# Attention and MLP in one kernel: more of v loaded, k copied and biased in another order, and a new plan of order and loads

## The chip, the cores and the metric

The kernel runs on one core of a Trainium2 chip. The metric is device time in microseconds (us) of one execution of the whole program; lower is better. The engines are TensorE (PE in the profile: matmuls), VectorE (DVE), ScalarE (ACT), GpSimd (POOL) and SyncE (SP). POOL and SP compute little here; they issue the DMAs, POOL the loads and SP the stores and the DMA transposes.

## The reference

Sliding-window attention feeds a two-layer MLP. Inputs and output are f32.

```python
# q, k, v: (8 batches, 8 heads, 576 positions, 64)
scores = (1 / 8) * q @ k.T                      # per batch and head
mask = (rel >= 0) & (rel < 64)                  # rel = query position - key position
attn = softmax(where(mask, scores, -1e9))
x = (attn @ v).transpose(0, 2, 1, 3).reshape(4608, 512)
h = x @ w_in                                    # 512 x 2048
return (h * sigmoid(h)) @ w_out                 # 2048 x 512
```

## The kernel before

**Attention** runs in blocks of 64 queries; a block needs its own 64 keys and the 64 before. A batch has 9 blocks, so there are 72 blocks and 18 units of 4 blocks. A unit goes through: scores on PE (L372 for units 0 to 4, L349 for the others), exponent on ACT (L378), mask on VectorE (L381; units 0 and 1 instead get a large negative bias, which PE adds before the scores with `window` or `window0` and `ident`, L363), values on PE ("pv", L412 or L400), reciprocal and norm on VectorE (L417, L420). Then the result is turned into `bridge`, the MLP's input with features on the partitions: for units in the set `BACK` by four PE transposes for each half (L436) and a copy (L439), for all others by a DMA transpose that SP issues (L430).

**The MLP** runs in 9 tiles of 512 tokens, two units to a tile. The first layer (L444) reads `bridge` and the whole of w_in, 8 loads of 256 columns each; ACT applies silu (L450). Tile 0 has a plain second layer (L513); tiles 1 to 5 have the second layer by seven products of sums (L517, sums of silu's output `gs` on VectorE, L505), and tiles 6 to 8 also the first layer (L481, with sums of `bridge`, L472). L878 adds up the output of tiles 1 and later.

**Loads.** All go through POOL's queue. q and k come for single units up to unit 4 (L297) and for half batches afterwards (L261, L274), with the positions on the partitions; VectorE turns them (L303, L316). For units 0 to 4 the keys of the block before are copied beside each block's own, 32 partitions at a time, by ACT or VectorE (`shift_k`, L292 and L294; r is the block of the unit). v needs 128 keys on the partitions for each block. Blocks 1, 3, 5, 7 and 8 of a batch are loaded so (`load_v`, L320, 128 KB each), and VectorE fills the even blocks from these (`shift_v`, L340 and L342). At most 8 loads are under way: POOL issues the next one when the one eight before it has landed. v has three buffers (NVB), so v of a batch waits until the batch three before is done with.

**The order** on every engine is fixed when the kernel is built. `Plan` simulates the engines with an estimated duration for each step, and at each moment gives a free engine the ready step of the lowest rank; each engine then executes the list that results, in order. `rank` gives each kind of step a number, `GO` says after how many MLP matmuls each unit's scores may come, and `SEQ` is the order of the first loads: a to e are k and q of units 0 to 4, v and y v of batches 0 and 1, w and o the eighths of w_in and w_out.

Of the kernel before, what the change touches and what calls it, by code (L numbers as in the profile page):

```python
# [124 lines left out]
def kernel(ctx, tc, q, k, v, w_in, w_out, out):  # L125
    nc = tc.nc
# [4 lines left out]
    NB = S // 64  # L131
# [10 lines left out]
    BACK = {0, 1, 2, 3, 5}  # L142
    GO = [52, 40, 40, 212, 232, 280, 393, 376, 440, 320, 585, 624, 56, 762, 352, 460]
# [7 lines left out]
    UP = 4  # L151
    LATE = [0, 0, 1, 3, 4, 4, 4, 4]
# [59 lines left out]
    def pair(op):  # L212
# [5 lines left out]
        rank=dict(one=-9, first=-9, late=5, dma=-1, st=-2, kshift=-0.5, xo=-20.9, turn=16.7, shift=34.1,  # L218
                  s=15.9, exp=-16.5, mask=9.4, pv=17.0, inverse=-18.6, norm=-28.3, ot=-1.2, bridge=-21.7,
                  silu=8.6, moe=99, warm=200, sum=4.1, xsum=-37.3, asum=15.9, plus=-31.0, stage=-0.9, wsum=7.8, piece=-29.3, out=-2.0, prime=-8,  # L220
                  turn2=-9.4, turn1=-26.9, shift0=-4.0, shift0b=27.1, shift1=36.9, inverse0=-5.3, norm0=-1.5, bridge0=16.8,),
# [34 lines left out]
    c_vv = [p.add("one", {"DVE": 0.4}, lambda _, i=i: clear_vv(i)) for i in range(NVB)]  # L256
    c_zero = p.add("one", {"DVE": 0.1}, lambda _: nc.vector.memset(zero, 0.0))
# [8 lines left out]
    def add_consts():  # L266
        c_ident = p.add("dma", {"POOL": 0.6}, const_ident)
        c_window = p.add("dma", {"POOL": 0.8}, const_window)
        c_window0 = p.add("one", {"DVE": 0.3}, const_window0, [c_window])
        return c_ident, c_window0, p.add("late", {"DVE": 0.8}, const_mask, [c_window])  # L270
# [48 lines left out]
    def load_v(b, t):  # L319
        nc.gpsimd.dma_start(  # L320
            out=vv[b % NVB][:, t, :, 0:D],
            in_=v[b, :, 64 * t - 64:64 * t + 64].rearrange("h s d -> s h d"),
        )
# [247 lines left out]
    def add_v(b, ts, shifts):  # L571
        users = pv_last.get(b - NVB, []) + [c_vv[b % NVB]]
        for t in ts:
            v_done[b, t] = [p.add("dma", {"POOL": 1.0}, lambda _, t=t: load_v(b, t), users,
                                  dma=0.9 if b < 2 else 1.35, late=1.5 * (t > 3) if b < 2 else LATE[b] + VLATE * (b > 2))]
        for low, a, z in shifts:
            n = len(range(a, z, 2))
            sh = p.add("shift", {"DVE": 0.1 + 0.22 * n}, lambda e, low=low, a=a, z=z: shift_v(e, b, low, a, z),
# [439 lines left out]
```

## Time and profile before

| | |
|---|---|
| median of 3 runs | 284.39 us (283.83, 284.39, 284.41) |
| the profiled execution | 283.85 us |
| its span in the profile | 282.1 us |
| mean granted clock of PE | 0.987 |
| busy: PE, VectorE, ACT, POOL | 272.2, 206.3, 172.7, 109.4 us |
| the chain that ended last | PE 85%, DMA 9%, POOL 2%, others 1% or less each |
| DMA | 32.52 MB in 106885 packets, 115 GB/s over the span |

A row of the timeline reads: start and length in us, engine, line, operation, output and inputs, how many instructions are taken together, and in brackets the idle time before them with what ended it. A row of the table by windows has the stretch, its length, the busy time of each engine with its count of instructions, PE's granted clock, the DMA engines' share and GB/s. Matmul ends are modelled, so a busy PE can hide short gaps. A page on DMAs gives for each kind of load the count, the size and the median from issue to landing.

### The profile page before, as it was taken

How to read it: one execution, taken by the hardware profiler on the slowest of the kernel's cores; microseconds unless marked ns; L12 is line 12 of the kernel's file. 1: busy time of each engine (PE TensorE's matmuls, PEld its weight loads, DVE VectorE, ACT ScalarE, POOL GpSimd, SP SyncE). 2: the span in 40 equal slices, each digit the busy share in tenths (PEclk: the TensorE clock that was granted, in tenths of full speed). 3: DMA queues.
4: the chain of work that ended last, by engine and by line, in shares of the span. 5: the costliest groups of instructions: out<-in, count | busy, mean ns of one | idle time of the engine just before them, and what ended most of it. 6: DMA issues, size and time to landing. Idle time of an engine off the chain costs nothing.

```text
span 282.1 us, 8326 instructions
## 1 busy us (share of the span) xinstructions
PE 272.2 (96%) x3509; PEld 192.9 (68%) x3509; DVE 206.3 (73%) x384; ACT 172.7 (61%) x266; POOL 109.4 (39%) x163
## 2 busy tenths in 40 slices
PE   8499999999999999999999999999999999999995
PEld 4376445545884478645875488547888888888884
DVE  5863468899967689797697657858587867868641
ACT  2486855786558686575847675666556664555631
POOL 8966847728998688873670000000000000000000
PEclk9869999999999999999999999999999999999999
DMA  8999999999999999999999202440013001201303
GB/s 82 155 195 189 185 185 184 199 245 137 131 197 181 147 130 163 171 190 129 144 158 197 40 0 78 121 69 0 2 37 99 16 22 66 67 0 40 114 30 119
DMA packets 106885, 32.52 MB, mean 115 GB/s; under 512 B 91488, under 2 KB 105824, under 8 KB 106848
## 3 DMA queue, kind: packets, MB, share of 16 engines
q0 software_dynamic: 83360, 19.15, 78.3%
q1 hardware_dynamic: 23488, 12.85, 20.8%
q8 instruction: 27, 0.44, 0.7%
q14 instruction: 10, 0.08, 0.1%
HBM read 38.27 MB, written 9.44 MB: 169 GB/s over the span
## 4 chain that ended last, share of the span: by engine, by line
PE 85%; DMA 9%; POOL 2%; issue 1%; ACT 1%; DVE 1%; POOLq 0%; DVEq 0%
PE mp L517 29%; PE mp L444 24%; PE la L481 8%; PE la L517 6%; PE mp L513 5%; PE mp L481 5%; DMA w_out_sb<-in_moe_w_out_dram 3%; PE at L349 3%; DMA nat<-in_k_dram 3%; PE at L400 3%; DMA nat<-in_q_dram 2%; PE at L412 1%; POOL nat L297 1%; PE at L372 1%; POOL vv L320 1%
## 5 line engine op out<-in xcount | busy, mean ns | idle before, releaser
L444 PE MATMUL mp<-bridge,w_in_sb 128*128 128x512 bf16 (+1 forms) x408 | 87.3, 367 | 0.8 <-issue 0.4
L450 ACT ACTIVATE gt<-mp 128x512 bf16<-128x512 f32 (+1 forms) x102 | 56.9, 573 | 24.2 <-PE mp L444 23.6
L444 PEld LDWEIGHTS <-w_in_sb 128*128 128x128 bf16 x408 | 38.7, 98 | 41.4 <-issue 1.4
L517 PEld LDWEIGHTS <-gs 128*128 128x128 bf16 x512 | 49.5, 98 | 5.9
L378 ACT ACTIVATE eo<-at 128x1024 bf16<-128x1024 f32 x34 | 33.6, 1026 | 14.1 <-PE at L349 8.7
L517 PE MATMUL mp<-ws,gs 128*128 128x256 bf16 x320 | 39.9, 273 | 0.0
L320 POOL DMA_DIRECT2D vv<-in_v_dram x40 | 35.6, 901 | 6.2 <-DMA nat<-in_k_dram 2.1
L517 PEld LDWEIGHTS <-gt 128*128 128x128 bf16 x288 | 27.5, 98 | 4.4
L274 POOL DMA_DIRECT2D nat<-in_q_dram x40 | 24.2, 623 | 15.6 <-DMA vv<-in_v_dram 9.1
L381 DVE TENSOR_TENSOR eo<-eo,mask 128x1024 bf16<-128x1024 bf16 x32 | 21.3, 677 | 8.0 <-ACT eo L378 7.9
L875 ACT COPY ot<-mp 128x512 f32<-128x512 f32 (+1 forms) x28 | 15.8, 563 | 18.6 <-PE mp L517 17.2
L274 POOL DMA_DIRECT2D nat<-in_k_dram x40 | 24.3, 628 | 3.8 <-DMA nat<-in_k_dram 1.3
L505 DVE TENSOR_TENSOR gs<-gt 128x1024 bf16<-128x1024 bf16 x24 | 16.5, 686 | 10.2 <-ACT gt L450 10.2
L492 ACT ACTIVATE eo<-vv 128x512 bf16<-128x512 f32 (+1 forms) x18 | 13.9, 773 | 16.2 <-DVE vv L766 16.2
L420 DVE TENSOR_TENSOR eo<-at,rc 128x512 bf16<-128x512 f32 x36 | 23.1, 670 | 0.2
L517 PE MATMUL mp<-w_out_sb,gt 128*128 128x256 bf16 x176 | 22.6, 273 | 0.0
L878 DVE TENSOR_TENSOR ot<-mp,ot 128x512 f32<-128x512 f32 (+1 forms) x21 | 13.8, 657 | 6.9 <-PE mp L517 5.7
L513 PE MATMUL mp<-w_out_sb,gt 128*128 128x512 bf16 x64 | 15.7, 380 | 0.0
L766 DVE TENSOR_TENSOR vv<-mp,vv 128x512 f32<-128x512 f32 x15 | 10.3, 688 | 7.1 <-PE mp L481 7.1
L766 DVE TENSOR_TENSOR vv<-la,vv 128x512 f32<-128x512 f32 x21 | 13.7, 682 | 2.0 <-PE la L481 1.7
L481 PEld LDWEIGHTS <-w_in_sb 128*128 128x128 bf16 x144 | 14.1, 98 | 1.6
L517 PE MATMUL mp<-w_out_sb,gs 128*128 128x256 bf16 x112 | 14.4, 273 | 0.0
(117 smaller groups left out, 397.1 us busy)
## 6 DMA issues: line engine op xcount, KB each, us to landing
out_dram<-ot SPq DMA_DIRECT2D x32, 256.0 KB, 3.6
vv<-in_v_dram POOLq DMA_DIRECT2D x40, 128.0 KB, 6.4
nat<-in_k_dram POOLq DMA_DIRECT2D x40, 72.0 KB, 5.4
nat<-in_q_dram POOLq DMA_DIRECT2D x40, 72.0 KB, 4.6
w_in_sb<-in_moe_w_in_dram POOLq DMA_DIRECT2D x8, 256.0 KB, 8.7
w_out_sb<-in_moe_w_out_dram POOLq DMA_DIRECT2D x8, 256.0 KB, 8.6
out_dram<-ot SPq DMA_DIRECT2D x8, 128.0 KB, 1.7
nat<-in_k_dram POOLq DMA_DIRECT2D x3, 256.0 KB, 6.3
```

Source lines behind the costliest of these rows:

```text
L274: nc.gpsimd.dma_start(out=nats[i].bitcast(BF16)[32 * r:32 * r + 32].rearrange("s (g y) -> s g y", y=128), in_=(q, k)[kk][b, h].rearrange(" ...
L320: nc.gpsimd.dma_start(out=vv[b % NVB][:, t, :, 0:D], in_=v[b, :, 64 * t - 64:64 * t + 64].rearrange("h s d -> s h d"),)
L378: nc.scalar.activation(out=dst, in_=src, func=ACTF.Exp, scale=scale)
L381: nc.vector.tensor_mul(es[w], es[w], mask)
L420: nc.vector.tensor_mul(oxs[o].rearrange("p x c (r d) -> p x (c r) d", r=2), at_pv(op, hf)[:, :, :, 0:D], rcs[r].unsqueeze(3).to_broadcast( ...
L444: nc.tensor.matmul(bank(bk)[:, lo:hi], lhsT=w_in_sb[:, c, ft * 128:(ft + 1) * 128], rhs=bridge[:, v0 + lo // 128:v0 + hi // 128, c], start ...
L450: nc.scalar.activation(out=gts[0][:, ft, lo:hi], in_=bank(bk)[:, lo:hi], func=ACTF.Silu)
L481: nc.tensor.matmul(bank(bk)[:, HT * f:HT * f + HT], lhsT=w[:, c, 128 * (2 * u + f):128 * (2 * u + f) + 128], rhs=rhs, start=first and f == ...
L505: (nc.vector.tensor_sub if i else nc.vector.tensor_add)(sums[i][:, f0:f1], x[:, f0:f1], y[:, f0:f1])
L513: nc.tensor.matmul(bank(bk), lhsT=gts[0][:, f, m * 128:(m + 1) * 128], rhs=w_out_sb[:, f], start=(f == 0), stop=(f == NFT - 1))
L517: nc.tensor.matmul(bank(bk)[:, HD * (m - m0):HD * (m - m0) + HD], lhsT=a[:, f, 128 * m:128 * m + 128], rhs=w[:, f], start=first and m == m ...
L766: d[k] = p.add("plus", {"DVE": 0.69}, lambda _: nc.vector.tensor_add(o, halves(bk), o), [op] + deps)
```

## The change

- From batch 4 on (`VB`) all 9 blocks of v are loaded, block 0 as a half load of 64 partitions, and nothing is copied between blocks. In batches 0 and 1 the copies may also run on ACT.
- The copies of k are planned in the order r = 1, 3, 0, 2, and 0 and 2 come after those that they would else cross; for unit 0 ACT makes 1 and 2, VectorE 3.
- `window0` is written by a memset on VectorE, without waiting for `window`, and a copy of its lower half on ACT. The constants come after k and q of units 0 and 1 in POOL's list, and the mask constant after the scores of unit 0.
- The bias of unit 1 waits for the scores of unit 0 and for k of unit 1.
- Unit 7 is turned on PE (`BACK`), and unit 4's values are one group (`SPLIT`).
- Ranks, `GO`, `SEQ` and some estimated durations have new numbers.

```diff
-    BACK = {0, 1, 2, 3, 5}
+    BACK = {0, 1, 2, 3, 5, 7}
-    SPLIT = (0, 1, 2, 3, 4)
+    SPLIT = (0, 1, 2, 3)
-    SEQ = "a v b v w w w w w o w y o w w c o d o v y o o e o o y".split()
+    SEQ = "a b v i v w w w w y o w w w v c w o o d y o o o e o o y".split()
+    VB = 4
...
-        rank=dict(one=-9, first=-9, late=5, dma=-1, st=-2, kshift=-0.5, xo=-20.9, turn=16.7, shift=34.1,
+        rank=dict(one=-9, first=-9, late=5, dma=-1, st=-2, kshift=-4.1, xo=-12.2, turn=19.0, shift=17.6,
...
     def const_window0(_):
-        nc.vector.tensor_copy(out=window0, in_=window)
-        nc.vector.memset(window0[0:64], -32768.0)
+        nc.scalar.copy(out=window0[64:128], in_=window[64:128])
...
+    c_low = p.add("one", {"DVE": 0.1}, lambda _: nc.vector.memset(window0, -32768.0))
...
     def load_v(b, t):
+        if t == 0:
+            nc.gpsimd.dma_start(out=vv[b % NVB][64:128, 0, :, 0:D], in_=v[b, :, 0:64].rearrange("h s d -> s h d"))
+            return
...
-                                  dma=0.9 if b < 2 else 1.35, late=...)]
+                                  dma=0.9 if b < 2 else 1.35 if b < VB else 0.95, late=...)]
...
-        sh = [p.add("kshift", {"ACT": 0.62, "DVE": 0.45}, lambda e, r=r: shift_k(e, u, r), [tk] + ([] if r else kb_done[u - 1][:1]),
-                    rank=-5.2 if u == 0 else p.rank["kshift"]) for r in range(4) if (4 * u + r) % NB]
+        sh, of = [], {}
+        for r in (1, 3, 0, 2):
+            if (4 * u + r) % NB:
+                of[r] = p.add("kshift", {"ACT": 0.62, "DVE": 0.55} if u else {"DVE": 0.5} if r == 3 else {"ACT": 0.62},
+                              lambda e, r=r: shift_k(e, u, r), [tk] + ([] if r else kb_done[u - 1][:1])
+                              + [of[x] for x in {0: (1,), 2: (1, 3)}.get(r, ()) if x in of],
+                              rank=-5.2 if u == 0 else p.rank["kshift"])
+                sh.append(of[r])
...
-            bi = p.add("bias", {"PE": 0.87}, lambda _: bias(u), [c_window0, c_ident] + kb_done[0][:1], ...)
+            bi = p.add("bias", {"PE": 0.95}, lambda _: bias(u), [c_window0, c_ident] + (s_new[0] + kb_done[1][:1] if u else []), ...)
...
+    c_mask["deps"].append(s_new[0][0])
...
-            add_v(b, ALL_V, ALL_S)
+            add_v(b, *((range(NB), ()) if b >= VB else (ALL_V, ALL_S)))
```

What the new plan does to the lists is seen in three places. The first is the start of POOL's list. nat are the landing places of k and q (70 and 71 for unit 0, 72 and 73 for unit 1), vv_82 is v of batch 0. Before:

```order
L297 DMA nat_70<-in_k_dram 128x8x128
L297 DMA nat_71<-in_q_dram 128x8x128
L228 MEMSET ident 128x128
L229 ISA
L229 AFFINE_SELECT ident<-ident 128x128
L233 MEMSET window 128x64
L234 AFFINE_SELECT window<-window 128x64
L236 AFFINE_SELECT window<-window 128x64
L320 DMA vv_82<-in_v_dram 128x8x64 x2
L297 DMA nat_72<-in_k_dram 128x8x128
L297 DMA nat_73<-in_q_dram 128x8x128
L320 DMA vv_82<-in_v_dram 128x8x64 x2
```

And after (line numbers are 2 to 13 higher in the changed kernel):

```order
L299 DMA nat_70<-in_k_dram 128x8x128
L299 DMA nat_71<-in_q_dram 128x8x128
L299 DMA nat_72<-in_k_dram 128x8x128
L299 DMA nat_73<-in_q_dram 128x8x128
L325 DMA vv_82<-in_v_dram 128x8x64 x2
L235 MEMSET window 128x64
L236 ISA
L236 AFFINE_SELECT window<-window 128x64
L238 AFFINE_SELECT window<-window 128x64
L230 MEMSET ident 128x128
L231 AFFINE_SELECT ident<-ident 128x128
L325 DMA vv_82<-in_v_dram 128x8x64 x2
```

k and q of unit 1 moved ahead of v and of the constants. The second place is what follows on POOL, up to k and q of unit 2 (nat 74 and 75, each in two pieces); vv_83 is v of batch 1. Before:

```order
L326 DMA w_in_sb<-in_moe_w_in_dram 128x4x256 x5
L332 DMA w_out_sb<-in_moe_w_out_dram 128x2x512
L326 DMA w_in_sb<-in_moe_w_in_dram 128x4x256
L320 DMA vv_83<-in_v_dram 128x8x64 x2
L332 DMA w_out_sb<-in_moe_w_out_dram 128x2x512
L326 DMA w_in_sb<-in_moe_w_in_dram 128x4x256 x2
L297 DMA nat_74<-in_k_dram 32x8x128
L297 DMA nat_74<-in_k_dram 96x8x128
L297 DMA nat_75<-in_q_dram 32x8x128
L297 DMA nat_75<-in_q_dram 96x8x128
```

And after:

```order
L331 DMA w_in_sb<-in_moe_w_in_dram 128x4x256 x4
L325 DMA vv_83<-in_v_dram 128x8x64 x2
L337 DMA w_out_sb<-in_moe_w_out_dram 128x2x512
L331 DMA w_in_sb<-in_moe_w_in_dram 128x4x256 x3
L325 DMA vv_82<-in_v_dram 128x8x64
L299 DMA nat_74<-in_k_dram 32x8x128
L299 DMA nat_74<-in_k_dram 96x8x128
L299 DMA nat_75<-in_q_dram 32x8x128
L299 DMA nat_75<-in_q_dram 96x8x128
L331 DMA w_in_sb<-in_moe_w_in_dram 128x4x256
L337 DMA w_out_sb<-in_moe_w_out_dram 128x2x512 x2
```

The eighth piece of w_in moved behind k and q of unit 2 and a v of batch 0, and ahead of w_out's second piece. The third place is on VectorE, where batch 7's k and q are turned (nat 76, 77, 70 and 71 into kt_81 and qt_79; the half batches come as 76 and 77, then 70 and 71); ot are output sums of tile 3, and rc_86 belongs to unit 12. Before:

```order
L316 STREAM_TRANSPOSE kt_81<-nat_76 128x9x2x32
L878 TENSOR_TENSOR ot_97<-mp_116,ot_97 128x512
L381 TENSOR_TENSOR eo<-eo,mask 128x1024
L384 MEMSET eo 64x4x32
L316 STREAM_TRANSPOSE qt_79<-nat_77 128x9x2x32
L878 TENSOR_TENSOR ot_96<-mp_115,ot_96 128x512
L381 TENSOR_TENSOR eo<-eo,mask 128x1024
L384 MEMSET eo 64x4x32
L316 STREAM_TRANSPOSE kt_81<-nat_70 128x9x2x32
L878 TENSOR_TENSOR ot_95<-mp_114,ot_95 128x512
L381 TENSOR_TENSOR eo<-eo,mask 128x1024
L417 RECIPROCAL rc_86<-at_111 128x8
```

And after:

```order
L890 TENSOR_TENSOR ot_96<-mp_113,ot_96 128x512
L318 STREAM_TRANSPOSE kt_81<-nat_76 128x9x2x32
L890 TENSOR_TENSOR ot_95<-mp_115,ot_95 128x512
L386 TENSOR_TENSOR eo<-eo,mask 128x1024
L422 RECIPROCAL rc_86<-at_111 128x8
L422 RECIPROCAL rc_87<-at_112 128x8
L425 TENSOR_TENSOR eo<-at_111,rc_86 128x512
L425 TENSOR_TENSOR eo<-at_112,rc_87 128x512
L386 TENSOR_TENSOR eo<-eo,mask 128x1024
L318 STREAM_TRANSPOSE qt_79<-nat_77 128x9x2x32
L422 RECIPROCAL rc_88<-at_111 128x8
L422 RECIPROCAL rc_89<-at_112 128x8
```

The first of these turns moved behind two of tile 3's output sums, and the later ones behind norms of units 12 and 13.

More of the change, by code (lines that the diff above doesn't have):

```diff
@@ L266, in add_consts @@
     def add_consts():
+        c_window = p.add("dma", {"POOL": 0.8}, const_window)
         c_ident = p.add("dma", {"POOL": 0.6}, const_ident)
[L268 to L269 removed]
+        c_window0 = p.add("prime", {"ACT": 0.25}, const_window0, [c_window, c_low], rank=-9)
         return c_ident, c_window0, p.add("late", {"DVE": 0.8}, const_mask, [c_window])
```

26 lines of the change are left out of this document (14 added, 12 removed).

## The prediction

> **What bounds the kernel now.** I read the page first, then busy time by stages, then TensorE's timeline up to 55 us, then the other engines where TensorE waits for them.
>
> ```profile
> PE 272.2 (96%) x3509; PEld 192.9 (68%) x3509; DVE 206.3 (73%) x384; ACT 172.7 (61%) x266; POOL 109.4 (39%) x163
> PE 85%; DMA 9%; POOL 2%; issue 1%; ACT 1%; DVE 1%; POOLq 0%; DVEq 0%
> ```
>
> TensorE (PE) is busy for 96% of the span and makes 85% of the chain that ended last; DMA's 9% lies at the start. So there are two places for a change of time: the start, where data are missing, and any later place where TensorE would newly wait. The stages of the start, with one stretch that loads only v and one late stretch (last columns: granted clock, DMA share, GB/s):
>
> ```profile
> 7.00:14.00 7.00, 3.57 (x104) 2.19 (x102) 5.55 (x10) 3.12 (x5) 6.67 (x10) 0.83 1.90 152
> 14.00:21.00 7.00, 6.56 (x129) 4.82 (x130) 4.39 (x11) 6.03 (x12) 4.67 (x7) 0.68 1.45 197
> 21.00:28.00 7.00, 6.70 (x53) 4.64 (x51) 2.34 (x6) 4.70 (x12) 4.24 (x7) 1.00 1.63 189
> 73.50:78.00 4.50, 4.50 (x69) 3.87 (x68) 4.45 (x10) 0.99 (x2) 4.50 (x8) 1.00 2.09 141
> ```
>
> From 7 to 14 us TensorE works half the time, and the loads run at 152 GB/s against 189 to 197 afterwards. TensorE's timeline:
>
> ```profile
> 9.87 0.68 PE L372 MATMUL at<-qt,kt 32*128 32x64 bf16 x64 [1.29 <-DVE qt L303]
> 22.70 11.43 PE L444 MATMUL mp<-bridge,w_in_sb 128*128 128x256 bf16 x64 [0.30 <-DVE bridge L439]
> 33.96 0.81 PE L513 MATMUL mp<-w_out_sb,gt 128*128 128x512 bf16 x3
> 35.03 0.68 PE L372 MATMUL at<-qt,kt 32*128 32x64 bf16 x64 [0.26 <-DVE qt L303]
> 35.65 4.71 PE L513 MATMUL mp<-w_out_sb,gt 128*128 128x512 bf16 x21
> 41.30 0.23 PE L372 MATMUL at<-qt,gs 32*128 32x64 bf16 x6 [0.38 <-issue]
> 53.66 2.54 PE L444 MATMUL mp<-bridge,w_in_sb 128*128 128x512 bf16 x11
> ```
>
> The second half of tile 0's first layer starts at 22.70 and runs without a gap to 33.96. The second layer then stops for 0.26 us (q of unit 2) and 0.38 us (scores of unit 3), and tile 1 starts at 53.66.
>
> **The start: when the last of w_in lands.** GpSimd (POOL) issues all loads; they land in that order.
>
> ```profile
> 4.41 1.80 POOL L320 DMA_DIRECT2D vv<-in_v_dram  x2
> 20.79 0.74 POOL L326 DMA_DIRECT2D w_in_sb<-in_moe_w_in_dram  x1 [0.57 <-DMA w_in_sb<-in_moe_w_in_dram]
> w_in_sb<-in_moe_w_in_dram POOLq DMA_DIRECT2D x1, 256.0 KB, 9.6
> ```
>
> The eighth w_in issues at 20.79 and lands 9.6 later, at 30.4. Ahead of it now stand k and q of unit 2 (512 KB) and one more v (128 KB), and w_out's second piece (256 KB) no longer: 384 KB more, at 189 GB/s 2.1 us later. Against that, k and q of units 0 and 1 go out first and together, with v and the constants behind. Before, v was issued at 4.41 ahead of the second k and q, and the queue ran slack: 7 us at 152 instead of 197 GB/s are 7 x (1 - 152/197) = 1.6 us. Part of the slack may be v itself (141 GB/s alone), so the bounds are 0 and 1.6; I take 1.4, since k and q come without a break now. w_in's last piece lands at 30.4 + 2.1 - 1.4 = 31.1. It feeds the last 8 matmuls of tile 0's first layer, 8 x 4.71/21 = 1.8 us: end at 33.0 with 0.1 for the handover, 1.0 earlier than 33.96.
>
> TensorE must be ready for that. The 64 matmuls from 22.70 take 11.3 us with all weights present, so the tile's second half may start as late as 21.7, 1.0 before today's 22.70. The copies of k make it early:
>
> ```profile
> 7.28 1.79 DVE L294 COPY kt<-kt 32x1024 bf16<-32x1024 bf16 x2 [0.68 <-ACT kt L292]
> 13.22 0.43 DVE L294 COPY gs<-gs 32x1024 bf16<-32x1024 bf16 x1 [0.40 <-ACT gs L292]
> 13.69 1.25 ACT L292 COPY gs<-gs 32x512 f32<-32x512 f32 x2 [0.49 <-DVE gs L294]
> ```
>
> ScalarE and VectorE wait for each other's copies: 0.68, 0.40 and 0.49 us. In the new order the copies of a unit read what their own engine wrote, or what is done. q of unit 0 is turned after one copy instead of two (0.9 less), so scores 0 come earlier than 9.87; so do scores 1, because k and q of unit 1 land before any v. v and the values of unit 0 come later, but the tile's second half hangs on unit 1. I put it at 22.70 less the three waits and the 0.30 for its bridge copy: 20.8, an estimate (bounds 20 and 22). Below 21.7 it costs nothing; at 22 it would cost 0.3. The second bias now waits for scores 0; behind it on TensorE stand only scores 1, which wait for their q longer.
>
> In the second layer of tile 0 the q of unit 2 is there, since it now lands ahead of w_in's last piece: the 0.26 goes. Unit 3's copies no longer cross engines, so the 0.38 can go; "issue" names no cause, so it may stay. I take 0.6 off, bounds 0.2 and 0.7 (w_out's pieces come within 0.2 of need). Start in all: 1.0 + 0.6 = 1.6 us earlier at tile 1.
>
> **Unit 7 turned on TensorE**: 8 transposes instead of two DMA transposes.
>
> ```profile
> 45.46 0.39 PE L436 MATMUL at<-ident,eo 128*128 128x128 bf16 x4
> 45.69 1.24 PE L513 MATMUL mp<-w_out_sb,gt 128*128 128x512 bf16 x5
> ```
>
> Four take 45.69 - 45.46 = 0.23 us of a full TensorE; eight cost 0.5. Nothing hides it.
>
> **v of batches 4 to 7 loaded whole**: 9 DMAs instead of 5 each, one of them half.
>
> ```profile
> L320 POOL DMA_DIRECT2D vv<-in_v_dram x40 | 35.6, 901 | 6.2 <-DMA nat<-in_k_dram 2.1 <-DMA w_out_sb<-in_moe_w_out_dram 0.8 <-issue 0.7
> nat<-in_k_dram POOLq DMA_DIRECT2D x1, 72.0 KB, 11.1
> 120.13 1.75 POOL L320 DMA_DIRECT2D vv<-in_v_dram  x2 [0.51 <-PE mp L444]
> 122.59 1.75 POOL L320 DMA_DIRECT2D vv<-in_v_dram  x2 [0.71 <-PE at L400]
> 124.46 0.62 POOL L274 DMA_DIRECT2D nat<-in_k_dram  x1
> 139.43 0.78 DVE L316 STREAM_TRANSPOSE kt<-nat 128x576 f32<-128x576 f32 x1 [0.23 <-PE at L349]
> 142.94 0.65 DVE L878 TENSOR_TENSOR ot<-mp,ot 128x512 f32<-128x512 f32 x1
> 145.68 0.67 DVE L381 TENSOR_TENSOR eo<-eo,mask 128x1024 bf16<-128x1024 bf16 x1
> 146.27 0.30 DVE L417 RECIPROCAL rc<-at 128x8 f32<-128x8 f32 x2
> 146.50 1.29 DVE L420 TENSOR_TENSOR eo<-at,rc 128x512 bf16<-128x512 f32 x2
> 145.56 0.70 PE L400 MATMUL at<-vv,eo 128*64 128x65 bf16 x32
> 148.78 0.70 PE L400 MATMUL at<-vv,eo 128*64 128x65 bf16 x32
> ```
>
> VectorE loses four copies per batch; it is not the bound, so that gains nothing. But POOL's queue gets 4 x 0.9 us more per batch, and the DMA 3.5 x 128 KB. k of batch 7 has the extra loads of batches 4, 5 and 6 ahead of it: 10.5 x 131 KB (decimal) at 141 GB/s = 9.8 us. Before, its first piece landed at 124.46 + 11.1 = 135.5 and, three of 72 KB later, all four by 137. New: 137 + 9.8 - 1.6 (earlier start) - 1.2 (POOL's waits of 0.51 and 0.71 for v buffers of batch 6, which a later queue no longer meets) = 144.0. It is needed thus: pv of unit 13 (148.78 before) comes at about 147.5, with TensorE 1.1 earlier and one matmul less ahead; on VectorE stand, in order behind the turn of that k, an output sum, a mask, and reciprocal and norm of unit 12: 0.78 + 0.65 + 0.67 + 0.30 + 1.29 = 3.7. So k must be there by 143.7. I charge 0.3 (bounds 0 and 2.6, below).
>
> **The rest** has one answer. Unit 4's values as one group instead of two, batch 0's and 1's v copies on either engine, the larger memset of the first bias and the new ranks move work on VectorE and ScalarE. TensorE's own order in the middle changes by a few matmuls.
>
> ```profile
> 118.00:134.00 16.00, 15.93 (x172) 8.32 (x174) 13.84 (x30) 10.67 (x19) 9.17 (x14) 1.00 2.12 159
> ```
>
> There TensorE is idle for 0.07 us in 16, with VectorE at 13.84: what these edits move lies beside TensorE and costs nothing. If the cover went, one late mask (0.67) would be its size. The late mask constant hides in front of unit 2 in the same way, since nothing before unit 2 reads it.
>
> **Sum.** The profiled execution took 283.85 us, 1.77 around its span. 283.85 - 1.6 + 0.5 + 0.3 = 283.0. The median of the runs shown lies 0.54 above the profiled one, so the time on that scale is 283.5.
>
> **Rivals.**
> *Late k (slower).* Place: VectorE's turn of batch 7's k, in front of unit 12's norm; point: landing after 143.7. If each of the 12 extra DMAs takes its 0.9 us of POOL and nothing absorbs it, it lands at 137 + 10.8 - 1.6 = 146.2: 2.5 us late, and TensorE waits that long at pv of unit 13. 283.5 - 0.3 + 2.5 = 285.7. For it: POOL's loads there wait for landings, so the queue is full. Against: before, the turn at 139.43 ran over 2 us after landing.
>
> *Late DMA transposes (slower).*
>
> ```profile
> bridge<-eo SPq DMA_TRANSPOSE x6, 9.5
> bridge<-eo SPq DMA_TRANSPOSE x6, 4.0
> 151.23 5.64 SPq L430 DMA_TRANSPOSE bridge<-eo  x4
> 156.63 0.42 DVE L472 TENSOR_TENSOR nat<-bridge 128x512 bf16<-128x512 bf16 x1 [0.88 <-issue]
> 163.35 0.69 DVE L505 TENSOR_TENSOR gs<-gt 128x1024 bf16<-128x1024 bf16 x1 [0.71 <-ACT gt L450]
> 165.14 3.45 PE L517 MATMUL mp<-ws,gs 128*128 128x256 bf16 x30
> ```
>
> Under full loads (120 to 131 us) a transpose lands after 9.5 us, from 147 on, with loads ending, after 4.0. Unit 13's second one goes at 152.5 - 1.1 = 151.4, now beside v of batch 7. With 9.5 it lands at 160.9; four sums L472 (1.5) and five L505 (5 x 0.69) follow: 165.9, where TensorE needs it by 165.4 - 1.1 = 164.3. 1.6 late: 283.5 - 0.3 + 1.6 = 284.8. It decides from a latency of 7.9. The Trainium skill, "DMA: Bandwidth & Descriptors" (Queues, rings and completion order), says that each DMA engine takes the queues in turn, packet by packet. By that a transpose would at most take twice its free time, 8.0, an estimate from that rule: 0.1 late, and this rival would be gone. The trace bears it out only in part: 9.5 against 4.0 is more than twice.
>
> *The queue stays slack.* Then w_in ends at 32.5, the first layer later than 33.96 by 0.4, and only the second layer gains: 283.5 + 1.4 = 284.9 at the worst bound, 284.2 with half of it.
>
> *Half clock on the first layer.* The granted clock was 0.83 and 0.68 in the two stretches up to 21 us, then 1.00. If the half-speed part moves 3 us later, it takes the 0.9 us of slack before w_in's last piece (20.8 against 21.7), and up to 0.6 more: 284.1. The Trainium skill, "TensorE: Matmul & The Clock Gate" (Part 1), has the rate set by a free-running window of about 3.4 us, so its phase is open; the rows show only where it lay once.
>
> *The copies still wait* (ScalarE's second copy reads what VectorE turned): first layer's half at 22.7 as today, start gain 0.6: 284.5.
>
> **Chances.** Forecast 0.48, late k 0.22, late transposes 0.10, slack queue 0.12, clock 0.04, copies 0.04. About 0.2%, 0.57 us, is what a measurement of this kernel can tell from no change. The forecast lies 0.9 below 284.39; 0.04 of it falls within 0.57, and 0.04 of the slack queue counts as faster: faster 0.48. Same: 0.04 + 0.08 + 0.02 (late k, little) + 0.04 + 0.04 = 0.22. Slower: 0.20 + 0.10 = 0.30. Range: from 282.3 (all 1.6 of the queue, 0.7 in the second layer, no late k: 282.9; and 0.6 for short gaps in the start that modelled matmul ends hide) to 286.0 (late k with its full bound). The forecast's own range is 282.3 to 284.0.
>
> **What would show it.** Right: first layer's end at 33.0, tile 1 at 52.1, k of batch 7 landing near 144. Wrong: w_in's eighth piece after 32; TensorE idle at L400 near 147 behind VectorE's L420, or at L517 near 164 behind L505.

## The result, and the profile after

The change makes the kernel slower. Its median is 286.94 us (284.69 to 293.61, 20 executions) against 284.13 (283.08 to 287.45, 20 executions on the same chip), the ratio 1.0076 with a 95% interval of 1.0052 to 1.0101. Ratios are formed from the executions within 1.5% of a kernel's fastest (13 of these 20), so where a kernel's times spread widely they say less than its median. The spread itself is new: 9 us, where 19 of the 20 executions of the kernel before lie within 2.1.

The profiled execution of the changed kernel took 286.79 us. Its engines and its chain, from the page:

```profile
PE 273.9 (96%) x3523; PEld 193.3 (68%) x3528; DVE 198.2 (70%) x366; ACT 174.4 (61%) x270; POOL 122.8 (43%) x179
PE 70%; DMA 15%; POOL 7%; issue 3%; DVE 2%; ACT 1%; POOLq 0%; DVEq 0%
L325 POOL DMA_DIRECT2D vv<-in_v_dram x52 | 46.0, 904 | 7.1 <-DMA w_out_sb<-in_moe_w_out_dram 1.9
```

TensorE's busy time rose by 1.7 us and the span by 2.9, but PE's share of the chain that ended last fell from 85% to 70%, and DMA and POOL together rose from 11% to 22%. POOL has 12 more whole loads of v (x52 for x40) and four half ones. TensorE's timeline at the start and at the one later place where it newly stands for long (start, length, then the idle time before the row in brackets):

```profile
19.09 10.86 PE L449 MATMUL mp<-bridge,w_in_sb 128*128 128x256 bf16 x64
32.05 3.36 PE L449 MATMUL mp<-bridge,w_in_sb 128*128 128x512 bf16 x8 [2.10 <-DMA w_in_sb<-in_moe_w_in_dram]
36.10 5.14 PE L518 MATMUL mp<-w_out_sb,gt 128*128 128x512 bf16 x22
54.20 2.10 PE L449 MATMUL mp<-bridge,w_in_sb 128*128 128x512 bf16 x9
168.71 2.58 PE L522 MATMUL mp<-ws,gs 128*128 128x256 bf16 x22 [1.92 <-DVE gs L510]
```

The second half of tile 0's first layer starts 3.6 us earlier than before (19.09 for 22.70), but then waits 2.10 us for w_in's last piece, and its last eight matmuls end at 35.4, where the whole layer ended at 33.96 before. Tile 1 starts at 54.20 (before 53.66). Much later, in tile 4's second layer, TensorE waits 1.92 us for sums of VectorE. VectorE's timeline at that place:

```profile
163.84 0.42 DVE L477 TENSOR_TENSOR nat<-bridge 128x512 bf16<-128x512 bf16 x1 [7.44 <-DMA bridge<-eo]
```

And the DMA transposes issued from 146 to 160 us, with their count and the median to landing:

```profile
bridge<-eo SPq DMA_TRANSPOSE x6, 8.6
```

The transposes land after 8.6 us (before 4.0), and the first sum that reads them (L477) has stood at the head of VectorE's list for 7.44 us; the `gs` sums for TensorE stand behind it. These are the transposes of units 12 and 13, whose sums serve tile 6; the expectations below call them tile 4's, after the second layer that waits for them.

A stage is taken from the first matmul of its line in the timeline to the first of the next stage. These are the stages in which the kernels below differ most, all times in us:

| kernel | median | profiled execution | tile 1 starts | tile 3's second layer | tile 4's second layer |
|---|---|---|---|---|---|
| before | 284.13 | 283.85 | 53.66 | 15.2 | 15.1 |
| changed | 286.94 | 286.79 | 54.20 | 15.1 | 17.2 |
| e1 sums moved | 287.12 | 287.50 | 52.83 | 19.2 | 15.1 |
| e2 w_in earlier | 286.52 | 284.53 | 52.96 | 16.2 | 15.2 |
| e3 filled wait | 290.98 | 290.80 | 53.36 | 22.4 | 16.0 |
| e4 no even loads | 283.20 | 282.75 | 53.14 | 15.1 | 15.1 |
| e5 sums and turns moved | 285.19 | 284.67 | 53.05 | 15.8 | 15.1 |
| e6 before, with loads | 296.88 | 298.77 | 53.44 | 17.0 | 16.7 |
| e7 copies, planned anew | 285.16 | 284.41 | 52.76 | 15.2 | 15.1 |
| e8 without batch 6's | 290.88 | 294.29 | 52.38 | 21.8 | 19.7 |
| e9 copies put back | 283.97 | 285.46 | 54.31 | 15.4 | 15.1 |
| e10 only 6 and 7 | 287.43 | 284.82 | 52.64 | 15.1 | 15.4 |
| e11 only 4 and 5 | 286.33 | 283.66 | 52.71 | 15.8 | 15.1 |
| e11, second profile | | 289.84 | 52.57 | 23.0 | 15.1 |
| e12 6 and 7, sums moved | 284.47 | 285.91 | 54.54 | 15.1 | 15.1 |
| e13 4 and 5, turns moved | 285.67 | 283.54 | 52.69 | 15.5 | 15.7 |

A second layer that TensorE need not wait in takes 15.1 to 15.2. Outside these stages TensorE also stands idle ahead of scores near 84 us (0.58 us in the changed kernel's profile, 1.22 in e10's, 1.26 in e9's, none in e4's) and near 110 us (0.92 in e10's). The trace puts these waits down to "issue" and so names no cause; e9 has its wait without any extra load. The kernel before, run again beside the experiments, had medians of 283.62 to 283.94.

### The profile page after: what moved, and what is told of

It reads as the page before. It is cut to its first block, busy times and chain, and to the rows that moved or that the text cites. A ratio compares the mean times of both kernels' runs of the same rounds, so it can differ in the third digit from the quotient of the medians.

```text
span 285.0 us, 8378 instructions
## 1 busy us (share of the span) xinstructions
PE 273.9 (96%) x3523; PEld 193.3 (68%) x3528; DVE 198.2 (70%) x366; ACT 174.4 (61%) x270; POOL 122.8 (43%) x179
## 4 chain that ended last, share of the span: by engine, by line
PE 70%; DMA 15%; POOL 7%; issue 3%; DVE 2%; ACT 1%; POOLq 0%; DVEq 0%
PE mp L522 24%; PE mp L449 17%; PE la L486 8%; PE la L522 6%; DMA w_in_sb<-in_moe_w_in_dram 6%; PE mp L518 5%; PE mp L486 5%; DMA vv<-in_v_dram 4%; DMA bridge<-eo 3%; POOL vv L325 3%; DMA nat<-in_q_dram 2%; PE at L354 2%; PE at L405 2%; POOL nat L276 1%; DVE gs L510 1%
## 5 line engine op out<-in xcount | busy, mean ns | idle before, releaser
L449 PE MATMUL mp<-bridge,w_in_sb 128*128 128x512 bf16 (+1 forms) x408 | 88.4, 371 | 2.5 <-DMA w_in_sb<-in_moe_w_in_dram 2.1
L455 ACT ACTIVATE gt<-mp 128x512 bf16<-128x512 f32 (+1 forms) x102 | 56.2, 573 | 25.9 <-PE mp L449 25.6
L325 POOL DMA_DIRECT2D vv<-in_v_dram x52 | 46.0, 904 | 7.1 <-DMA w_out_sb<-in_moe_w_out_dram 1.9
L887 ACT COPY ot<-mp 128x512 f32<-128x512 f32 (+1 forms) x28 | 15.7, 562 | 20.8 <-PE mp L522 19.7
L497 ACT ACTIVATE eo<-vv 128x512 bf16<-128x512 f32 (+1 forms) x18 | 13.8, 773 | 16.2 <-DVE vv L778 16.2
L518 PE MATMUL mp<-w_out_sb,gt 128*128 128x512 bf16 x59 | 14.6, 380 | 0.5 <-issue 0.3
```

Of the source, the lines that this page charges most:

```text
L325: nc.gpsimd.dma_start(out=vv[b % NVB][:, t, :, 0:D], in_=v[b, :, 64 * t - 64:64 * t + 64].rearrange("h s d -> s h d"),)
L449: nc.tensor.matmul(bank(bk)[:, lo:hi], lhsT=w_in_sb[:, c, ft * 128:(ft + 1) * 128], rhs=bridge[:, v0 + lo // 128:v0 + hi // 128, c], start ...
L455: nc.scalar.activation(out=gts[0][:, ft, lo:hi], in_=bank(bk)[:, lo:hi], func=ACTF.Silu)
L518: nc.tensor.matmul(bank(bk), lhsT=gts[0][:, f, m * 128:(m + 1) * 128], rhs=w_out_sb[:, f], start=(f == 0), stop=(f == NFT - 1))
```

## The experiments

Line numbers shift by 2 to 8 between the experiments' kernels; the operations and names stay the same.

### e1 to e4: each wait by itself, and all the extra loads

**e1** moves, in the finished list of VectorE, the four sums that read those transposes (class `xsum`) behind the eight `gs` sums of tile 4. Nothing else moves.

```diff
+        xs = [i for i, (op, e) in enumerate(order) if op["cls"] == "xsum"][:4]
+        last = [i for i, (op, e) in enumerate(order) if op["cls"] == "sum" and i > xs[-1]][7]
+        moved_ops = [order[i] for i in xs]
+        order = [o for i, o in enumerate(order[:last + 1]) if i not in xs] + moved_ops + order[last + 1:]
         self.order = order
```

> The changed kernel, with the four sums of bridge (L472 of before) moved behind the eight sums of gs of tile 4 in VectorE's list; nothing else moves. Theory A (the late DMA transposes stop TensorE only because VectorE takes its steps in order): TensorE's wait of 1.9 us at L517's second sum near 166 us is gone, the transposes land as late as before (about 163.7), and the time falls by 1.9 to 2.1 us, to about 284.5. Rival B (the full DMA queue costs everywhere): the wait moves to another place, the time falls by less than 0.7 us. The start is as in the changed kernel in both.

Measured: 287.12 us (284.15 to 290.89), ratio 1.0077 (1.0048 to 1.0106). The wait it was aimed at is gone (15.1 in tile 4), which this profile alone does not put down to the move, since e11's second profile (below) has a free tile 4 behind a late tile 3 without it; e12 does. The time is not lower, because in this profile another wait stands one tile earlier. VectorE there:

```profile
132.78 0.78 DVE L322 STREAM_TRANSPOSE kt<-nat 128x576 f32<-128x576 f32 x1 [4.01 <-DMA nat<-in_k_dram]
133.48 0.65 DVE L514 TENSOR_TENSOR gs<-gt 128x1024 bf16<-128x1024 bf16 x1
136.17 0.78 DVE L322 STREAM_TRANSPOSE qt<-nat 128x576 f32<-128x576 f32 x1
```

And TensorE in tile 3's second layer:

```profile
137.58 4.66 PE L526 MATMUL mp<-ws,gs 128*128 128x256 bf16 x28 [2.06 <-DVE gs L514]
```

VectorE stands for 4.01 us at the turn of batch 6's second k, which has not landed; the sums for tile 3's second layer (L514) come behind it, with one more turn among them, and TensorE waits 2.06 us for these.

**e2** issues the eighth piece of w_in ahead of w_out's first piece, nothing else.

```diff
+        wo = next(i for i, (op, e) in enumerate(order) if op.get("w") == "o0")
+        order.insert(1 + next(i for i, (op, e) in enumerate(order) if op.get("w") == "w7"), order[wo])
+        del order[wo]
...
```

> The changed kernel, with the first piece of w_out issued behind the eighth piece of w_in; nothing else moves on POOL or any other engine. Theory A (tile 0's first layer ends when w_in's last piece lands, and an idle TensorE loses its clock): the piece lands 1.3 us earlier, at 30.7, the idle time before the last eight matmuls falls from 2.1 to 0.8 us, the half clock that follows goes (3.4 us for eight becomes 1.8), and the first layer ends near 32.6 instead of 35.3. The second layer then waits for pieces of w_out, up to 1 us; tile 1 starts 1.5 to 2.8 us earlier. Rival B (the second layer is bound by w_out's later pieces anyway): the first layer ends earlier, but tile 1 starts within 0.5 us of the changed kernel's 54.2.

Measured: 286.52 us (284.14 to 291.50), ratio 1.0070 (1.0040 to 1.0100). The timeline shows that what the first layer wins, the second layer gives back:

```profile
30.98 1.90 PE L452 MATMUL mp<-bridge,w_in_sb 128*128 128x512 bf16 x8 [0.30 <-DMA w_in_sb<-in_moe_w_in_dram]
39.26 0.20 PE L380 MATMUL at<-qt,gs 32*128 32x64 bf16 x2 [0.69 <-ACT eo L386]
39.95 0.67 PE L380 MATMUL at<-qt,gs 32*128 32x64 bf16 x62 [0.49 <-ACT gs L297]
```

The first layer ends at 32.8 instead of 34.0 to 34.4 (e1, e4), but the scores of unit 3 then wait 0.69 and 0.49 us, and tile 1 starts at 52.96, where e1 has 52.83. The late piece of w_in alone is not what tile 1 waits for.

**e3** lets TensorE run 12 matmuls on `blank` ahead of the last eight of tile 0's first layer, to keep the clock up over the wait.

```diff
+        if j == 0 and ft == 14 and c == 0:
+            for _ in range(12):
+                nc.tensor.matmul(bank(bk)[:, 0:384], lhsT=blank[:, 0:128], rhs=blank, start=True, stop=True)
```

> The changed kernel, with twelve matmuls of zeros (128x384) on TensorE ahead of the last eight matmuls of tile 0's first layer, in the time in which TensorE waits for w_in's last piece. Theory A (the clock is halved because TensorE stood idle): the granted clock stays at 1.0, the eight matmuls take 1.8 instead of 3.4 us, tile 1 starts 1.5 us earlier. Rival B (the clock falls for another reason, or the eight wait for something else): the eight still take over 3 us, or the time is longer by the 1.9 us of added matmuls.

Measured: 290.98 us (289.69 to 292.23, 6 executions), ratio 1.0251 (1.0220 to 1.0282). The eight matmuls took their full-speed time:

```profile
32.83 1.89 PE L452 MATMUL mp<-bridge,w_in_sb 128*128 128x512 bf16 x8
```

But e4 has the same after an idle wait:

```profile
32.51 1.90 PE L451 MATMUL mp<-bridge,w_in_sb 128*128 128x512 bf16 x8 [1.97 <-DMA w_in_sb<-in_moe_w_in_dram]
```

And e9 (below), with the same wait, takes nearly twice as long:

```profile
32.12 3.54 PE L455 MATMUL mp<-bridge,w_in_sb 128*128 128x512 bf16 x8 [1.95 <-DMA w_in_sb<-in_moe_w_in_dram]
```

So the half clock after this wait comes in some executions only: the mean granted clock from 30 to 36 us is 0.72 in the profiles of the changed kernel and of e9, and 1.00 in e4's. e3 does not price it. Its profile loses the time in tile 3's second layer, 22.4 us, behind VectorE's waits of 2.64 and 2.87 us at q and k of batch 6; why all six of its executions take this long is open.

**e4** leaves out the 16 even loads of v in batches 4 to 7, so that the even blocks hold older data; the order is that of the changed kernel.

```diff
     def load_v(b, t):
+        if b >= VB and t in (0, 2, 4, 6):
+            return
```

> The changed kernel without the loads of blocks 2, 4 and 6 and the half load of block 0 of v in batches 4 to 7, so even blocks hold older data there; every other instruction stands in the same order. Theory A (the 16 extra loads keep the queue full when unit 13 is turned by DMA): the fourth transpose lands before 158, TensorE's wait near 166 us is gone, and the time falls by about 2 us; nothing else changes by over 0.5 us. Rival B (the transposes are late for another reason, such as their own number or the loads of k and q): they land after 160 and the wait stays over 1 us.

Measured: 283.20 us (282.24 to 285.19), ratio 0.9982 (0.9960 to 1.0004). By medians the extra loads cost 286.94 - 283.20 = 3.7 us (3.6 when each is first set against the kernel before as it ran beside it), by ratios 1.0076 - 0.9982 = 0.9%, 2.7 us. Both waits are gone; TensorE's first matmuls on `gs` in tile 3 and in tile 4 have no idle time ahead of them:

```profile
133.11 0.27 PE L524 MATMUL mp<-ws,gs 128*128 128x256 bf16 x1
...
164.24 3.00 PE L524 MATMUL mp<-ws,gs 128*128 128x256 bf16 x26
```

And the transposes of 146 to 160 us land fast:

```profile
bridge<-eo SPq DMA_TRANSPOSE x6, 2.9
```

The rest of the change is worth at most a few tenths of a percent: the interval just reaches 1.

### e5 to e8: is it VectorE's order, and which loads?

**e5** adds to e1's move a second one: the last three turns of batch 6 go behind the eight sums of tile 3.

```diff
+        sums_ = [i for i, (op, e) in enumerate(order) if op["cls"] == "sum"][16:24]
+        ts = [i for i, (op, e) in enumerate(order) if op["cls"] == "turn" and i < sums_[-1]][-3:]
+        late_turns = [order[i] for i in ts]
+        order = [o for i, o in enumerate(order[:sums_[-1] + 1]) if i not in ts] + late_turns + order[sums_[-1] + 1:]
```

> The changed kernel with two moves on VectorE alone: the four sums that read the DMA transposes of tile 4 stand behind tile 4's other eight sums (as in e1), and the last three turns of batch 6 (q of its first half, k and q of its second) stand behind the eight sums that tile 3's second layer reads, in place of ahead of and between them. The 16 extra loads of v stay. Theory A (the extra loads make batch 6's k and q late, and the loss comes only because VectorE works in order, so that the sums behind the waiting turns are late too): the second layer of tile 3 takes 15.1 to 15.3 us again and that of tile 4 too, 283.2 to 284.2 us, the level of e4 and a little. Theory C (the loads themselves are late for the scores that need them, so that the wait only moves to the scores of batch 6): both second layers 15.1 to 15.3, but the first-layer stage of tile 4 or the scores in it longer by 2 to 4 us, 286 to 288. Theory B (the loss lies in other parts of the change): no change, 286.5 to 287.5.

Measured: 285.19 us (283.10 to 288.92), ratio 1.0043 (1.0016 to 1.0071). Between the expectations: with all loads in place 1.8 us of the median come back, 1.2 when each kernel is set against the one before as it ran beside it (2.8 and 1.6 us above it). The intervals of the two ratios overlap, so the size of this gain is uncertain. Both second layers are near free with the turns behind the sums, so nothing in them needed batch 6's k and q so early. The profile shows a third wait, VectorE at batch 7's k:

```profile
146.62 0.81 DVE L326 STREAM_TRANSPOSE kt<-nat 128x576 f32<-128x576 f32 x1 [4.02 <-DMA nat<-in_k_dram]
```

and TensorE at values behind a norm:

```profile
149.46 0.44 PE L413 MATMUL at<-vv,eo 128*64 128x65 bf16 x16 [1.19 <-DVE eo L433]
```

**e6** puts the extra traffic alone into the kernel before: 16 loads of v of the same shape, between those of batches 4 to 7, to memory that nothing reads.

```diff
+        if b >= 4 and t < 8:
+            nc.gpsimd.dma_start(out=dump[:, (4 * b + t // 2) % 8], in_=...)   # 128 positions of v, as above
```

> The kernel before with only the extra traffic of the change: four more loads of v, of the same shape, in each of batches 4 to 7 (16 in all), written to memory that nothing reads, between the loads of v that are there. Order of all other instructions as before. Theory A (the extra loads are the price): 286 to 289 us, with the second layer of tile 3 longer than 15.2 us behind a late turn of batch 6. Theory B (the loss lies in how the change orders its instructions, and the loads are harmless in an order with more slack): under 284.8, no second layer longer than 15.4.

Measured: 296.88 us (294.76 to 301.53, 6 executions), ratio 1.0446 (1.0401 to 1.0490). The loads alone cost 296.88 - 283.62 = 13.3 us in the kernel before, over three times the price in the changed one. The wait is of the same kind, one stage earlier, in tile 3's first layer, which takes 28.1 us instead of 17.0. VectorE stands at the turn of batch 6's k:

```profile
128.92 0.78 DVE L317 STREAM_TRANSPOSE kt<-nat 128x576 f32<-128x576 f32 x1 [10.21 <-DMA nat<-in_k_dram]
```

A norm that TensorE needs is behind it:

```profile
130.57 1.25 PE L406 MATMUL at<-vv,eo 128*64 128x65 bf16 x32 [8.99 <-DVE eo L426]
```

**e7** sets `VB = 8` in the changed kernel: copies in all batches as before, the rest of the change kept, planned anew.

> The changed kernel with VB = 8 in place of 4: even blocks of v are copied on chip in all batches as before, everything else of the change stays, and the planner puts the copies into its order. It computes the whole result. Theory A: 282.8 to 283.8 us (e4, which left the loads out, had 283.2; the copies run on VectorE beside TensorE's work), ratio to before 0.996 to 1.000. Theory B: 285.5 or more, since the order of the change stays.

Measured: 285.16 us (283.99 to 286.54), ratio 1.0050 (1.0030 to 1.0070). The expectation failed, and not for the reason that theory B had. The spread is narrow again and both second layers are free, but the planner, given the copies, also moved two exponentials of ScalarE in between the activations of tile 3. ScalarE:

```profile
119.30 1.28 ACT L383 ACT_TABLE_LOAD   x1 [0.19 <-issue]
120.59 1.94 ACT L383 ACTIVATE eo<-at 128x1024 bf16<-128x1024 f32 x2
122.55 1.28 ACT L455 ACT_TABLE_LOAD   x1
```

And TensorE behind it:

```profile
124.49 1.89 PE L449 MATMUL mp<-bridge,w_in_sb 128*128 128x512 bf16 x8 [1.47 <-ACT gt L455]
```

Two tables more are loaded, and TensorE waits 1.47 us. An experiment that has the planner run again tests more than its edit.

**e8** leaves out the four even loads of batch 6 alone (`b == 6` in e4's edit).

> The changed kernel without the four even loads of v of batch 6 alone (batch 6's even blocks of v are left out of the result's data); the other 12 extra loads stay. Theory A1 (batch 6's own loads delay batch 6's second k and q, which follow within microseconds, and this is most of the price): 283.5 to 284.8, tile 3's second layer at 15.1 to 15.4, what is left being tile 4's wait on its DMA transposes. Theory A2 (the queue has been getting later since batch 4, all 16 loads count alike): a quarter of the 3.7 us of e4 is won, 285.8 to 286.3.

Measured: 290.88 us (285.57 to 295.43, 6 executions), ratio 1.0107 (1.0050 to 1.0164): no gain, and its profile waits in both second layers, in tile 4's behind a wait of VectorE of 9.50 us at the transposes of units 12 and 13. Both expectations fell. That its median lies above the changed kernel's, with four loads fewer, is not explained. Batch 6's own loads stand behind its k and q in POOL's list, so they could not delay these; those of batches 4 and 5 stand ahead.

### e9: the copies put back without a new plan

The order of e4, and the 16 copies inserted in VectorE's list at the place where the planner takes their loads to have landed. It computes the whole result.

```diff
...
+        for op, e in getattr(self, "extra", []):
+            put(dict(op, at=max(d["seen"] for d in op["deps"])), e, max(d["seen"] for d in op["deps"]))
...
```

> A whole kernel again: the order of the changed kernel as in e4, without the 16 extra loads, and the 16 copies on VectorE put back one by one at the place where the planner takes their loads to have landed; nothing else moves. In e7 the planner, given the copies, also moved two exponentials of ScalarE between the activations of tile 3, and TensorE waited 1.5 us there. If the copies lie beside TensorE's work as in the kernel before: 283.0 to 284.0 us, ratio 0.997 to 1.001. If VectorE has no room for their 9 us in this order (0.42 to 1.1 us each, ahead of normalizations and sums that TensorE waits for): 284.5 to 286.

Measured: 283.97 us (282.95 to 285.46), ratio 1.0001 (0.9982 to 1.0020). VectorE has the room, the wide spread does not come back, and the kernel is level with the one before. None of the kernels here that compute the whole result is faster than the one before by more than its interval.

### e10 to e13: two halves, two waits

**e10** leaves out the even loads of batches 4 and 5 only, **e11** those of 6 and 7 only (`b in (4, 5)` and `b in (6, 7)` in e4's edit).

> The changed kernel without the even loads of v of batches 4 and 5 alone (their even blocks are left out of the result's data); those of batches 6 and 7 stay. In the traces so far the loads of batches 4 and 5 stand ahead of batch 6's k and q in GpSimd's queue, those of 6 and 7 behind. Theory A3 (the eight extra loads of batches 4 and 5 push batch 6's k and q into the stretch from 115 us on, where transfers that take 5 us elsewhere take 7 to 10): 283.2 to 284.6, tile 3's second layer at 15.1 to 15.3 us. Theory A2 (all 16 count alike): half of the 3.7 us of e4 is won, 285 to 285.5, and the wait in tile 3's second layer is still there. Theory B (order): 286.5 or more.

> The other half: the changed kernel without the even loads of v of batches 6 and 7 alone (their even blocks are left out of the result's data); those of batches 4 and 5 stay, and batch 6's k and q are as late as in the changed kernel. Theory A3: 285.8 to 288.5, with waits of VectorE on nat and of TensorE on gs in tile 3's second layer or just behind it in the profile; only the wait on tile 4's DMA transposes gets shorter, since the loads of batch 7 are beside those. Theory A2: 285 to 285.5. A result under 284.3 would say that the loads of batches 6 and 7 are the price.

Measured: e10 287.43 us (283.69 to 290.83), ratio 1.0047 (1.0014 to 1.0080); e11 286.33 us (283.66 to 294.07), ratio 1.0054 (1.0028 to 1.0080). Theory A3 fell with e10, theory A2 too: either half alone costs most of what both do (by ratios 0.65% and 0.72% over e4, against 0.94%, with intervals that overlap). Each half was then given the one move that takes away the wait which theory D assigns to it: **e12** is e10 with e1's move, **e13** is e11 with the turns of e5. Both halves were also run once more for a second profile.

> The kernel of e10 (even loads of v of batches 4 and 5 left out, those of 6 and 7 there), and on VectorE the four sums that read tile 4's DMA transposes moved behind tile 4's other eight sums, as in e1. Theory D (two waits, one of each half; with the loads of batches 6 and 7 it is the wait on tile 4's transposes): 283.2 to 284.6 us, and a narrow spread, all runs below 286.5. Theory E (another wait, or any extra load disturbs the queue at places that change from run to run): as e10, 286.5 to 288 with runs over 288.

> The kernel of e11 (even loads of v of batches 6 and 7 left out, those of 4 and 5 there), and on VectorE the last three turns of batch 6 moved behind the eight sums that tile 3's second layer reads, as in e5. Theory D (with the loads of batches 4 and 5 it is the wait on batch 6's late k and q): 283.4 to 285 us, all runs below 287, tile 3's second layer 15.1 to 15.4. Theory E: as e11, 285.5 to 287 with runs over 290.

> e10 once more, for a second profile (even loads of v of batches 4 and 5 left out). If its time is over 286.5: by theory D tile 4's second layer is over 15.5 us behind the sums that read its transposes, and tile 3's is at 15.1 to 15.3; by theory E the lost time lies elsewhere.

> e11 once more, for a second profile (even loads of v of batches 6 and 7 left out). If its time is over 285.5: by theory D the lost time lies in tile 3's second layer or the first-layer stage of tile 4 behind late turns of batch 6, and tile 4's second layer is at 15.1 to 15.3; by theory E elsewhere.

Measured for e12: 284.47 us (282.75 to 285.92), ratio 1.0012 (0.9989 to 1.0035). Moving four sums takes 3.0 us off e10's median and 4.9 off its highest time, as theory D has it (its two bounds, 284.6 and 286.5, hold). The transposes are as slow as ever, but what stands behind them is no longer awaited. e12's VectorE:

```profile
162.34 0.69 DVE L516 TENSOR_TENSOR gs<-gt 128x1024 bf16<-128x1024 bf16 x1 [5.89 <-ACT gt L461]
168.46 0.42 DVE L483 TENSOR_TENSOR nat<-bridge 128x512 bf16<-128x512 bf16 x1
```

And its transposes from 146 to 160 us:

```profile
bridge<-eo SPq DMA_TRANSPOSE x6, 9.0
```

The second profile of e10 is of 283.88 us, an execution with little to wait for (15.8 in tile 4's second layer), so the wait in e10's longest executions is concluded from what its removal did and was not seen itself.

e13: 285.67 us median, ratio 1.0044 (1.0015 to 1.0074), nine of its 12 executions below 286.6, two at 287.4 and 288.8, and one of 561.2, which nothing here explains. The highest times of e11 (290.6 to 294.1) are gone but for that one, yet the median misses the expected 285, three executions lie above the expected 287, and the ratio hardly moves (e11 1.0054). So for this half theory D is not borne out by the time: another price remains, and e13's profile, its fastest execution, does not show it. The second profile of e11, 289.84 us, shows one of its longest executions, with the wait in theory D's place. VectorE:

```profile
134.04 0.78 DVE L318 STREAM_TRANSPOSE kt<-nat 128x576 f32<-128x576 f32 x1 [3.39 <-DMA nat<-in_k_dram]
```

TensorE:

```profile
135.45 0.28 PE L524 MATMUL mp<-ws,gs 128*128 128x256 bf16 x1 [2.99 <-DVE gs L512]
138.76 5.80 PE L524 MATMUL mp<-ws,gs 128*128 128x256 bf16 x28 [1.98 <-DVE gs L512]
```

The stretch from 130.5 to 145.5 us as a window (busy time of PE, weight loads, VectorE, ScalarE, POOL; granted clock, DMA share, GB/s):

```profile
130.50:145.50 15.00, 10.03 (x126) 7.20 (x128) 8.03 (x13) 5.58 (x7) 10.79 (x17) 0.77 2.06 138
```

Tile 3's second layer takes 23.0 us, 7.9 over a free one. Waiting is 5.0 of that; the remainder is clock. The 28 matmuls behind the second wait take 5.80 us, 207 ns each, where e4's 26 take 3.00, 115 ns each; the granted clock over the stretch is 0.77. POOL's timeline says why that k is so late. The last q of batch 6 in e4:

```profile
113.18 2.38 POOL L276 DMA_DIRECT2D nat<-in_q_dram  x4
```

And in this execution:

```profile
130.03 0.60 POOL L276 DMA_DIRECT2D nat<-in_q_dram  x1 [2.10 <-DMA nat<-in_q_dram]
```

In e4 batch 6's k and q are all issued by 115.6. With eight loads more ahead of them they still stand in the list after 115, when DMA transposes and stores run beside them (that these are what slows the loads is not tested); the loads of k issued from 110 to 124 us took 10.0 us in the median to land (4.3 to 5.0 for batch 6's k in e4), and POOL, with eight loads under way, waits for one to land before it issues the next.

## Why the prediction was wrong

**The step that failed is the cover of the 16 extra loads of v.** I followed their delay to one consumer, k of batch 7, and charged 0.3 us; I gave 0.10 to late transposes, with a decision point, and asked nothing of batch 6. The range, too, let only one consumer be late at a time, where e8's profile has two. Measured, the loads cost 2.7 to 3.7 us (e4) through three waits of one kind: VectorE, in order, stands at an instruction whose data are late, and sums or norms for TensorE stand behind it. They are the transposes of units 12 and 13 (shown in the changed kernel's profile, and by e1 and e12), batch 6's second k and q ahead of tile 3's sums (e1, e5, e11's second profile), and batch 7's k (e5's profile). The first is the rival as it was written: 8.6 us to landing against its decision point of 7.9, TensorE idle at the `gs` matmuls behind `nat<-bridge` sums, 1.92 us against the 1.6 worked out. The third is the other rival at its named place, and in the changed kernel's own profile it does not show: there k of batch 7 was turned at 144.81 with no idle time before it.

```profile
144.81 0.77 DVE L318 STREAM_TRANSPOSE kt<-nat 128x576 f32<-128x576 f32 x1
```

The second stood in no case of mine, and it is the largest: 4 us in e1, 7.9 in e11's second profile.

**The bound of a packet-by-packet queue.** The Trainium skill, "DMA: Bandwidth & Descriptors" (Queues, rings and completion order), has the queues served in turn, from which I estimated at most 8.0 us for a transpose, twice its free time. The prediction's own rows, 9.5 against 4.0, already stood against that estimate, and it should not have counted against the rival. The runs have 8.4 (e10), 8.6 and 9.0 us beside loads of batch 7, against 4.0 before and 2.9 in e4: two to three times. The measurement decides; serving in turn does not by itself bound the latency at twice. e11, which issues none of the extra loads in that stretch but batch 7's five other loads of v and one of q, has 7.6 us: loads there go with slow transposes whether they are the extra ones or others that came late. Stores alone do not: e9's transposes took 2.4 us beside three stores.

**One queue delay is not a sum of independent terms.** The 9.8 us of delay were followed to one place. That k did land near the forecast 144.0, at 143.5, but by luck: it was issued 9.2 us later than before (133.61 for 124.46), where the sum had 9.8 - 1.6 - 1.2 = 7.0, and landed after 6.2 to 9.1 us, not 11.1. What counts is which loads the delay moves into the stretch from 115 to 135 us, where the medians for k lie between 7.0 (changed kernel) and 11.9 us (e10), against 4.3 to 5.0 for batch 6's k in e4. e4 puts v of batch 6 and the first k and q of batch 7 there, which are needed later; the changed kernel puts k and q of batch 6 there. How far they are caught varies between executions of one kernel: e11's two profiles have 15.8 and 23.0 us in tile 3's second layer. That this makes the wide spread fits, but is not shown beyond these two. That the two halves do not add may come from a tile that waits giving the next tile's transposes time; in e1 and e11's second profile tile 4 is free where tile 3 waits, but e8 waits in both, so this is argued and not shown.

**The start: 1.6 us forecast at tile 1, 0.5 found in e4 and up to 1.3 in the other profiles at full clock** (53.14 in e4 and 52.38 in e8 against 53.66). The first layer, forecast 1.0 earlier, ends at 33.6 (e8) to 34.3 (e4) where 33.96 stood before. From there to tile 1 the second layer takes 18.8 us for 19.7, a gain of 0.9 where I had 0.6. The queue's slack was mis-sized: w_in's last piece landed at 31.7 (e8) to 32.4 (e4), not at 31.1, so the slack regained was 0.1 to 0.8 us and not 1.4, which is the slack-queue rival in part. The changed kernel's row for the stretch shows why:

```profile
7.00:14.00 7.00, 5.68 (x171) 3.14 (x171) 5.83 (x11) 5.49 (x11) 6.81 (x12) 1.00 2.07 170
```

The loads run at 170 GB/s there, where 152 stood before and the sum had 197: 7 x (170 - 152)/197 = 0.6 us. e2 adds that an earlier piece does not help, as the second layer then waits for unit 3's scores. TensorE was early enough, as forecast (19.09 against an estimate of 20.8). In the changed kernel's profile the wait of 2.10 us also cost clock: 3.36 us for eight matmuls that take 1.90 at full speed, so tile 1 came 0.5 later than before.

**Unit 7 on TensorE, and the rest at nothing.** From tile 1 to tile 3 e4 takes 61.25 us (61.37 before): TensorE is busy 0.25 us longer (61.18 for 60.93), within the 0.5 forecast, and the 0.44 us that it stands idle there before, put down to "issue", is gone. Behind tile 4's second layer e4 takes 104.1 us for 104.5, a gain that no term had; TensorE is busy for 101.03 us of it in both, and no run separates its cause. So e4's span, 281.0 for 282.1, meets the forecast less its charge for k (-1.6 + 0.5 = -1.1) by luck: it is 0.5 from the start, 0.1 up to tile 3 and 0.4 behind tile 4.

## What to carry to other kernels

A load that nobody waits for still costs its place in the queue: list everything behind it, and for each ask which engine will stand at it in order, and what stands behind that. A delay in a queue was priced here by what it moved into the queue's slow stretch, not by its length alone. And a change that takes away the slack shows first in the spread of the times: look at several executions before trusting one profile's wait as the cause.

## What the runs showed that I had not expected

Waits of about 2 us lower TensorE's clock in some executions and not in others: with 1.95 to 2.10 us of idle time in the same place, eight matmuls took 1.90 us (e4, granted clock 1.00 from 30 to 36 us), 3.36 (changed, 0.72) and 3.54 (e9, 0.72); e10's took 1.90 after 2.25 us of idle time. What decides it is open. So a 2 us wait may cost 2 or 3.6 us, and in e11's second profile 5.0 us of waits cost 7.9. The Trainium skill, "TensorE: Matmul & The Clock Gate" (Part 1), has the clock fall after an idle window of about 3.4 us; here it was down after single waits of 1.95 (e9) and 2.10 us (the changed kernel), both shorter than that.
